# Emformer attention and a pyramid-residual MoE on one core: the first round of dense tiles in two parts

## The chip, the cores and the metric

The kernel runs on one core of one Trainium2 chip. A core has five engines with queues of their own: TensorE (PE, matrix products, with a weight load before each), VectorE (DVE), ScalarE (ACT), GpSimd (POOL) and SyncE (SP). DMA queues are fed by SP, ACT and POOL and share 16 DMA engines. Products are written to PSUM, of which the kernel uses eight banks; everything else on the chip lies in SBUF. The metric is the device time in microseconds of one execution; the kernel before takes 242.95 us, the median of three runs (242.71 to 243.45).

## The reference

```python
def reference(**kwargs):
    attn_out = _attn_ref(q, k, v, mem_k, mem_v)      # (4, 8, 768, 64)
    x = attn_out.transpose(0, 2, 1, 3).reshape(3072, 512)
    return _moe_ref(x, ...)

# attention: 24 chunks of 32 queries; each sees 8 memory keys, 16 keys to the left,
# its own 32 and 8 to the right
scores = scale * np.matmul(q_c, k_full.transpose(0, 1, 3, 2))
a = np.exp(scores - scores.max(-1)); a = a / (a.sum(-1) + 1e-09)
out[:, :, c_start:c_end] = np.matmul(a, v_full)

# MoE: 3072 tokens, width 512, 8 experts of hidden width 512, one expert per token
y_dense = np.maximum(x @ w1_dense, 0.0) @ w2_dense
expert_idx = np.argmax(x @ w_gate, axis=1)
y_moe[mask] = gate_w[mask, None] * (np.maximum(x[mask] @ w1[e], 0.0) @ w2[e])
return y_dense + y_moe
```

`gate_w` is the softmax probability of the chosen expert. All inputs are float32; the kernel loads q, k and the MoE weights as bfloat16.

## The kernel before

**Attention.** The work goes by pairs of heads: 16 pairs `i`, four to a batch `b`. For a pair PE transposes q and k (`transpose_qk`, done two pairs ahead), computes scores of the next pair, transposes the probabilities back (`probs_back`), and multiplies them with the values (`values`, in two halves). DVE takes the maximum and the difference, ACT the exponential; `scaled` (L446) divides by the row sums and so gives x. `gate_part` transposes x (in two PSUM banks), `gate_sum` multiplies it with the gate's weights, `gate_add` sums over the pairs of a batch, and `record` (ACT) writes x as bfloat16 into the batch's records. Values lie in a window layout that needs two copies per pair (`copy_v`, one for each head), on POOL and on DVE or ACT.

**Routing.** When a batch's four pairs are summed, `logits`, `choose`, `ranks` and `rank` find each token's expert and its row in that expert's region of a DRAM tensor `x_reg` (3200 rows for each of 8 experts); `rows_out` (L585, POOL, indirect DMA) writes six times 128 rows there. This runs one or two pairs behind the attention of the next batch. `fill_out` writes 128 pad rows at the start of each region.

**First round.** After three batches at least 11 tiles of 128 rows are whole within their expert. `list_a` (L626, some dozen small DVE steps over 8 counts or 11 x 8 fields) finds where they start and writes it to `src_i`; `bases` (L178) has SP read the list into registers, and `fetch` (L188) has SP load a tile of rows. `transposed` (L199) transposes it on PE into a PSUM bank and copies it on DVE to `xT_of`; `dense_first` (L213, L227) and `dense_second` (L230) are the dense layers, with ACT emptying their banks. In the kernel before, the list stands in pair 15, ahead of that pair's values; the first tile's transposes come after batch 3's logits.

**Second round and experts.** After batch 3's rows `list_b` makes 16 more tiles (20 at most) from the remainders; they go the same way (tiles 11 to 26). Then every tile gets its expert's first layer (`expert_first`, weights copied by DVE to `w_st`, L942) and second layer (`expert_second`, L950), and `out` rows are written by indirect DMA (L964). Seven first layers go ahead of the first second layer, which needs all of `w2_all`.

**Orders.** The order on each engine is written out by hand (`manual_schedule`): instructions of an engine run in the order in which the code issues them, and waits are put in from the data. PSUM tiles named "tp" (`bank`, L101) are two banks used in turn by q and k transposes, `gate_part`, `logits`, `ranks`, `ends` and `transposed`: whoever takes one waits for the reader of the one two before. SP's queue is in order: a fetch that waits holds the fetches behind it. POOL's queue holds weight loads, row writes and copies in order; weights for the second layers are loaded two at a time, the next when the one before the last has landed (L973 to L979), in space that attention's tiles free.

## Time and profile before

| | |
|---|---|
| median of 3 runs | 242.95 us (242.71 to 243.45) |
| the profiled execution's own time | 238.85 us |
| its span | 237.0 us |
| PE busy | 195.5 us, 82% |
| PE weight loads | 146.3 us, 62% |
| DVE busy | 157.2 us, 66% |
| ACT busy | 135.0 us, 57% |
| POOL busy | 145.1 us, 61% |
| DMA | 59879 packets, 38.57 MB |

The profile is of one execution. Its page gives busy times, the span in 40 slices (each digit the busy share in tenths), the chain that ended last and the costliest groups of instructions. A timeline row has start and length in microseconds from the span's start, the engine, the line in the kernel's code, the operation, the tiles written and read, the count, and in brackets the idle time before it and what ended it. "issue" means that nothing the profile shows was waited for. PEld is the weight load, which runs beside products; a queue of an engine has a q behind its name. The first half of the slices is attention, with DMA and DVE near full; from about 129 us on PE is.

### The profile page before, as it was taken

The page shows a single profiled execution, that of the slowest core. Times are in us where ns is not written, and L with a number is a line of the kernel's source. Part 1 is how long each engine was busy: PE and PEld are TensorE (multiplying, and loading weights), DVE is VectorE, ACT ScalarE, POOL GpSimd, SP SyncE. Part 2 cuts the span into 40 slices and gives each one's busy share as a digit, 9 for nine tenths or more (in the row PEclk, how much of TensorE's full clock was granted, in tenths as well). Part 3 has the DMA queues.
Part 4 walks back from the last instruction along what each step waited for, and adds up shares of the span by engine and source line. Part 5 has one row for each costly group of instructions (what it writes and reads, how often), then busy time and mean ns, then how long its engine had stood idle before and what let it go on. Part 6 is the DMA issues. An engine that isn't in the chain of part 4 may idle for free.

```text
span 237.0 us, 7850 instructions
## 1 busy us (share of the span) xinstructions
PE 195.5 (82%) x3147; PEld 146.3 (62%) x3147; DVE 157.2 (66%) x372; ACT 135.0 (57%) x205; POOL 145.1 (61%) x215
## 2 busy tenths in 40 slices
PE   0578787988887888696568999999999899999960
PEld 0467665756666667564336777777778766666630
DVE  4587999879877999877735652222244478888750
ACT  7256676996879678987313555555556433322220
POOL 7939996418996599958312841121232079888880
PEclk9999999999999999999959999999999999999995
DMA  5999999999999999999888569999999324433331
GB/s 87 184 204 129 158 156 188 168 141 166 136 210 206 164 171 198 188 165 278 156 202 140 148 100 250 232 183 187 170 163 148 52 93 175 177 136 127 150 146 76
DMA packets 59879, 38.57 MB, mean 163 GB/s; under 512 B 35646, under 2 KB 57534, under 8 KB 59840
## 3 DMA queue, kind: packets, MB, share of 16 engines
q0 software_dynamic: 21584, 25.20, 58.1%
q1 hardware_dynamic: 37216, 11.77, 28.5%
q10 hardware_dynamic: 1040, 1.06, 1.5%
q8 instruction: 27, 0.44, 0.8%
q14 instruction: 12, 0.10, 0.2%
HBM read 43.22 MB, written 11.30 MB: 230 GB/s over the span
## 4 chain that ended last, share of the span: by engine, by line
POOL 23%; DMA 20%; issue 9%; PE 5%; DVE 5%; ACT 4%; POOLq 1%; ACTq 0%; DVEq 0%
DMA w_all<-in_moe_w_dram 16%; POOL out_dram L964 12%; POOL x_reg L589 5%; POOL idle L583 4%; DMA x_reg<-rec,row_i 2%; DMA xg<-x_reg 2%; PE sc L218 1%; ACT kbd L379 1%; DVE dif L417 1%; DVE mx L411 1%; DVE x L450 1%; DVE kbd L378 1%; ACT qT L374 1%; PE tp L470 1%; PE av L438 1%
## 5 line engine op out<-in xcount | busy, mean ns | idle before, releaser
L589 POOL DMA_INDIRECT x_reg<-rec,row_i x24 | 26.7, 1111 | 20.7 <-ACT rec L480 12.5
L964 POOL DMA_INDIRECT out_dram<-y,dst_i x27 | 29.0, 1074 | 14.3 <-DVE y L960 10.6
L438 PE MATMUL av<-vw,at 128*32 128x130 f32 x768 | 29.1, 284 | 8.5 <-issue 3.9
L438 PEld LDWEIGHTS av<-vw,at 128*32 128x32 f32 x768 | 20.7, 112 | 15.6 <-issue 6.5
L218 PEld LDWEIGHTS <-w_st 128*128 128x128 bf16 x432 | 25.5, 98 | 5.8 <-DVE w_st L942 3.2
L224 ACT ACTIVATE h<-sc 128x512 bf16<-128x512 f32 x27 | 16.1, 597 | 22.8 <-PE sc L218 22.8
L353 POOL COPY vw<-vw 24x1536 f32<-24x1536 f32 x15 | 22.5, 1499 | 9.7 <-DMA vw<-in_v_dram 9.1
L218 PEld LDWEIGHTS <-w1d 128*128 128x128 bf16 x432 | 26.2, 100 | 2.2 <-issue 1.8
L942 DVE COPY w_st<-w_all 128x2048 bf16 x27 | 19.9, 740 | 5.6 <-PE sc L218 4.1
L224 ACT ACTIVATE xT_B<-sc 128x512 bf16<-128x512 f32 x16 | 9.6, 597 | 23.5 <-PE sc L218 23.5
L422 ACT ACTIVATE a<-dif 128x768 f32<-128x768 f32 x16 | 13.5, 845 | 16.0 <-DVE dif L417 13.8
L207 DVE COPY xT_B<-tp 128x512 bf16<-128x512 bf16 x16 | 6.8, 425 | 23.4 <-PE tp L204 23.2
L378 DVE COPY kbd<-tp 64x768 bf16<-64x768 bf16 x16 | 15.2, 948 | 8.0 <-PE tp L365 7.9
L977 POOL CAST scratch<-w_all 1x1 f32<-1x1 bf16 x10 | 1.7, 174 | 28.8 <-DMA w_all<-in_moe_w_dram 28.8
L234 PE MATMUL av<-w2d,h 128*128 128x512 bf16 x72 | 18.5, 379 | 0.0
L430 ACT COPY at<-at_ps 128x768 f32<-128x768 f32 x16 | 12.8, 799 | 7.8 <-PE at_ps L428 7.6
L218 PE MATMUL sc<-xT_B,w_st 128*128 128x128 bf16 x256 | 16.9, 219 | 0.2 <-DVE w_st L942 0.2
L218 PE MATMUL sc<-xT_B,w1d 128*128 128x128 bf16 x256 | 16.9, 219 | 0.0
L411 DVE TENSOR_REDUCE mx<-sc 128x12 f32<-128x768 f32 x16 | 15.3, 956 | 1.7 <-PE sc L401 1.4
L417 DVE TENSOR_TENSOR dif<-sc,mx 128x768 f32<-128x768 f32 x16 | 15.3, 958 | 1.6
L473 ACT COPY xT<-tp 128x384 f32<-128x384 f32 x32 | 13.9, 490 | 3.7 <-PE tp L470 3.7
L450 DVE TENSOR_TENSOR x<-av,rs 128x768 f32<-128x768 f32 x16 | 15.3, 958 | 0.6
(160 smaller groups left out, 449.0 us busy)
## 6 DMA issues: line engine op xcount, KB each, us to landing
w_all<-in_moe_w_dram POOLq DMA_DIRECT2D x14, 512.0 KB, 7.7
vw<-in_v_dram SPq DMA_DIRECT2D x30, 200.0 KB
xg<-x_reg SPq DMA_DIRECT2D x27, 129.0 KB
q_bf<-in_q_dram POOLq DMA_DIRECT2D x16, 192.0 KB, 7.8
k_bf<-in_k_dram POOLq DMA_DIRECT2D x16, 192.0 KB
vw<-in_mem_v_dram SPq DMA_DIRECT2D x32, 48.0 KB
x_reg<-fill ACTq DMA_DIRECT2D x1, 1032.0 KB
w_all<-in_moe_w_dram POOLq DMA_DIRECT2D x4, 256.0 KB, 6.8
```

The lines of the kernel that those rows point to most:

```text
L218: written(place, nc.tensor.matmul(ph[:, f, :], w[:, d, f * 128:(f + 1) * 128], xT[:, d, :], start=(d == 0), stop=(d == DT - 1),))
L224: was_read(place, nc.scalar.activation(h_sb, ph, AF.Relu))
L234: written(place, nc.tensor.matmul(pd, h_d[:, f, :], w2d_sb[:, f, :], start=(f == 0), stop=(f == FT - 1)))
L353: copy(vt[p0 + CHUNK:p0 + CTX, :NCH, hh, :D], vt[p0:p0 + n, 1:, hh, :D])
L378: lo = nc.vector.tensor_copy(dst[:D, 0], srcv[:D])
L411: nc.vector.reduce_max(mx, scv, axis=AX.X)
L417: nc.vector.tensor_tensor(dif.rearrange("p (b t) (h k) -> p b (t h) k", b=2, h=2), scv, mx.to_broadcast([128, 2, T, KEYS]), ALU.subtract,)
L438: nc.tensor.matmul(av[cc * CHUNK:(cc + 1) * CHUNK, t // TB, (t % TB) * W2:(t % TB + 1) * W2], at[:, t, cc * CHUNK:(cc + 1) * CHUNK], vt[:, ...
L450: nc.vector.tensor_tensor(x_p.rearrange("p (b t) (h d) -> p b (t h) d", b=2, h=2), avv[:, :, :, :D], rs.to_broadcast([128, 2, TB * 2, D]), ...
L589: inst = nc.gpsimd.indirect_dma_start(x_reg, bass.IndirectOffsetOnAxis(ap=row_i[:, t:t + 1], axis=0), rec[:, t, :], None,)
L942: nc.vector.tensor_copy(w_st[:, None], w1_all[:, bass.ds(e_dve.pop(s), 1), :, :])
L964: inst = nc.gpsimd.indirect_dma_start(out, bass.IndirectOffsetOnAxis(ap=dst_i[:, s:s + 1], axis=0), y, None, bounds_check=N_tokens - 1, oo ...
```

## The change

- The first round comes in two parts. `list_a` becomes `whole_tiles`, called twice. The first call uses the counts after two batches and gives N1 = 5 tiles; its steps stand in pairs 10, 11 and 12, and the rest of them at the start of pair 15. SP fetches these five in pair 13, before batch 2's row writes in the code, with no order between those rows and these loads. The second call, after pair 15's products, gives tiles 5 to 10.
- `fill_out`'s rows and the fetches of whole tiles have no order between them any more.
- Tiles 0 and 1 are transposed in pair 15 between `probs_back` and `gate_part`; first layers of tiles 0 to 4 stand between the last products of attention and gate, tile 5's transposes and tile 0's second layer ahead of batch 3's ranks. Second layers run three tiles behind the first ones in the first round, and the round's last three end before tile 11.
- `choose` no longer stands behind tile 0's copy on DVE but behind tile 4's; the list is behind `scaled` of the last pair instead of ahead of it.
- The first copy of values for pair 15 moves from ACT in pair 14 to POOL in pair 13, between batch 2's row writes.
- Weights are loaded with four neighbouring rows to a partition, one piece of 8 KB of float32, instead of four rows 128 apart; to match, transposes and first layers read every fourth column. Two weight loads of expert first layers move from the chain at the end to places ahead of and between batch 3's row writes.
- Eight buffers instead of six for fetched tiles, six instead of three for h.

```diff
-    NA, NB, NFIX = 11, 20, 16
+    N1, NA, NB, NFIX = 5, 11, 20, 16
-    m_load = ctx.enter_context(tc.tile_pool(name="m_load", bufs=6))
+    m_load = ctx.enter_context(tc.tile_pool(name="m_load", bufs=8))
...
+    def load_rows(src_ap, dst):
+        nc.gpsimd.dma_start(dst, src_ap.rearrange("(p t) m -> p t m", p=128))
...
-        if s < NA:
-            load_insts.append(inst.ins)
-            for r in row_insts:
+        for b in ((2, 3) if s < N1 else (3,) if s < NA else ()):
+            load_insts[b].append(inst.ins)
+            for r in row_insts[b]:
                 tc.declare_no_dep(
...
+        xk = xgb[:, :D_moe].rearrange("p (m k) -> p k m", k=DT)
         for d in range(DT):
-            nc.tensor.transpose(
-                xtp[:, d, :], xgb[:, d * 128:(d + 1) * 128], identity
-            )
+            nc.tensor.transpose(xtp[:, d, :], xk[:, d, :], identity)
...
+        wk = w.rearrange("p d (m k) -> p d k m", k=FT)
...
-                    ph[:, f, :], w[:, d, f * 128:(f + 1) * 128], xT[:, d, :],
+                    ph[:, f, :], wk[:, d, f, :], xT[:, d, :],
...
-            h_sb = m_work.tile([128, FT, 128], BF16, tag="h", name="h")
+            h_sb = m_work.tile([128, FT, 128], BF16, tag="h", name="h", bufs=6)
...
-    def list_a():
+    def whole_tiles(before, n, cum, first, at):
         cnt = ends()
         ni = r_work.tile([128, E], I32, tag="ni", name="ni")
         nc.vector.tensor_copy(ni, cnt)
+        yield
...
+        yield
...
-        nc.vector.tensor_tensor(src_i[:, :NA], bs, base_a, ALU.add)
+        nc.vector.tensor_tensor(src_i[:, at:at + n], bs, first, ALU.add)
         yield
...
+        if at == 0:
+            nc.vector.tensor_tensor(whole1, reg25, d1[:, :E], ALU.add)
+            nc.vector.tensor_scalar(lim1, whole1, 128.0, None, ALU.mult)
+            step = r_work.tile([128, E], F32, tag="step", name="step")
+            nc.vector.tensor_tensor(step, d1[:, 1:], d1[:, :E], ALU.subtract)
+            nc.vector.tensor_scalar(jump1, step, 128.0, float(ROWS), ALU.mult, ALU.add)
+            nc.vector.scalar_tensor_tensor(
+                base1, d1[:, :1].to_broadcast([128, NA]), 128.0, base_a,
+                op0=ALU.mult, op1=ALU.add,
+            )
...
+            if i == NPAIR - 1:
+                for _ in parts:
+                    pass
...
             probs_back(i)
+            if i == NPAIR - 1:
+                transposed(0)
+                transposed(1)
             gate_part(i - 1)
...
-        if i == NPAIR - 1:
-            parts = list_a()
+        values(i, range(TB))
+        if i in (11, 12):
             next(parts)
-            bases(0, 6)
-            for s in range(6):
-                fetch(s)
-            bases(6, NA)
-        values(i, range(TB))
...
+        if i == NPAIR - 1:
+            dense_first(0)
         if i:
             record(i - 1)
-            if i == NPAIR - 2:
-                copy_v(i + 1, 0, nc.scalar)
...
+        if i == 10:
+            parts = whole_tiles(reg25, N1, cum1, base_a[:, :N1], 0)
+            next(parts)
...
         if i == NPAIR - 3:
-            while rows_todo:
+            bases(0, N1)
+            for s in range(N1):
+                fetch(s)
+            for t in range(T):
                 row_out()
-                if rows_todo:
+                if t == T // 2 - 1:
+                    copy_v(NPAIR - 1, 0, nc.gpsimd)
+                elif t < T - 1:
                     pause()
-            load_w(*w_todo.pop(0))
+            next_w()
...
     last_p = NPAIR - 1
+    next_w()
+    dense_first(1)
     scaled(last_p)
     gate_add(last_p - 1)
+    parts = whole_tiles(whole1, NA - N1, cumA, base1[:, :NA - N1], N1)
+    next(parts)
+    transposed(2)
+    next(parts)
+    next(parts)
+    bases(N1, NA)
+    for s in range(N1, N1 + 3):
+        fetch(s)
     gate_part(last_p)
-    nc.gpsimd.tensor_copy(scratch, xg_of[1][0:1, 0:1])
-    load_w(*w_todo.pop(0))
+    dense_first(2)
+    transposed(3)
+    record(last_p)
     gate_sum(last_p)
-    record(last_p)
     gate_add(last_p)
+    dense_first(3)
+    for s in range(N1 + 3, NA):
+        fetch(s)
+    transposed(4)
     logits(B - 1)
-    transposed(0)
-    dense_first(0)
     choose(B - 1)
-    transposed(1)
-    fetch(6)
-    dense_first(1)
+    dense_first(4)
+    nc.gpsimd.tensor_copy(scratch, xg_of[N1 + 1][0:1, 0:1])
+    next_w()
+    transposed(N1)
+    dense_second(0)
     ranks(B - 1)
     rank(B - 1)
     for t in range(T):
         rows_out(B - 1, (t,))
-        if t < T - 1:
+        if t == T // 2 - 1:
+            next_w()
+        elif t < T - 1:
             pause()
-    dense_second(0)
...
-    for s in range(3, NA):
-        if 4 <= s and s + 5 < NA:
-            fetch(s + 5)
-        if 5 <= s + 1 < NA:
+    for s in range(N1, NA):
+        dense_first(s)
+        if s + 1 < NA:
             transposed(s + 1)
-        dense_first(s)
-        dense_second(s - 1)
-        if s == 5:
+        dense_second(s - 3)
+        if s == N1 + 1:
+            next(parts)
+        if s == N1 + 2:
             for _ in parts:
                 pass
+    for s in range(NA - 3, NA):
+        dense_second(s)
```

`next_w` is `load_rows(*w_todo.pop(0))`. In the second round `dense_second(s - 1)` is left out for the first tile, since the round before has done it.

102 lines of the change are left out of this document (52 added, 50 removed).

## The prediction

> **What bounds the kernel now.** I read the page's head and slices, then busy time by stretch, then the timelines of TensorE (PE), the queues and VectorE (DVE) around the joint of attention and experts.
>
> ```profile
> span 237.0 us, 7850 instructions
> PE   0578787988887888696568999999999899999960
> ```
>
> ```profile
> 118.60:122.00 3.40, 1.72 (x8) 0.48 (x6) 0.42 (x1) 0.75 (x2) 0.00 (x0) 0.50 1.11 229
> 122.00:125.40 3.40, 2.78 (x24) 2.58 (x25) 1.50 (x8) 0.27 (x1) 1.04 (x3) 0.50 0.64 153
> 129.00:146.00 17.00, 17.00 (x208) 12.92 (x207) 8.05 (x45) 9.81 (x17) 9.97 (x20) 1.00 0.70 139
> 150.00:180.00 30.00, 30.00 (x356) 22.31 (x354) 8.47 (x41) 18.14 (x31) 7.34 (x16) 1.00 1.03 177
> ```
>
> The columns are stretch, length, busy PE, weight loads, DVE, ScalarE, GpSimd, granted clock, DMA share and GB/s. From 129 us on PE is full: the end hangs on when it fills and on what is left by then. Before that lies a hole, the slices of 6, 5 and 6, with two stretches at clock 0.50.
>
> ```profile
> 122.10 0.61 PE L204 MATMUL tp<-identity,xg 128*128 128x128 bf16 x4 [1.26 <-DMA xg<-x_reg]
> 123.22 1.86 PE L218 MATMUL sc<-xT_A,w1d 128*128 128x128 bf16 x16 [0.52 <-DVE xT_A L207]
> ...
> 147.00 0.40 PE L204 MATMUL tp<-identity,xg 128*128 128x128 bf16 x4 [0.35 <-DMA xg<-x_reg]
> 147.23 1.06 PE L218 MATMUL sc<-xT_B,w1d 128*128 128x128 bf16 x16
> 148.12 1.03 PE L234 MATMUL at_ps<-w2d,h 128*128 128x512 bf16 x4
> 148.99 0.39 PE L204 MATMUL tp<-identity,xg 128*128 128x128 bf16 x4
> ...
> 188.04 1.02 PE L955 MATMUL av<-w_all,xT_A 128*128 x4 [1.10 <-issue]
> ...
> 228.12 1.02 PE L955 MATMUL at_ps<-w_all,xT_B 128*128 x4
> ```
>
> Start to start, a tile's transposes take 0.23 us, its first dense layer 0.89, its second 0.87. PE waits at 122.10 for tile 0 and at 147.00 for tile 12: both times for rows that went out to x_reg and back. The last product ends at 229.14, the span 7.9 later.
>
> ```profile
> 118.25 0.38 SPq L190 DMA_DIRECT2D xg<-x_reg  x1
> ...
> 139.89 0.33 SPq L190 DMA_DIRECT2D xg<-x_reg  x1
> ```
>
> ```profile
> 128.74 1.04 POOL L589 DMA_INDIRECT x_reg<-rec,row_i  x1 [4.86 <-ACT yd_A L237]
> ...
> 136.26 0.97 POOL L589 DMA_INDIRECT x_reg<-rec,row_i  x1 [0.17 <-issue]
> 137.24 1.62 POOL L115 DMA_DIRECT2D w_all<-in_moe_w_dram  x2
> ...
> 179.73 0.75 POOL L115 DMA_DIRECT2D w_all<-in_moe_w_dram  x1 [0.28 <-issue]
> ```
>
> So a chain is behind PE's second wait: batch 3 routed, six row writes (128.74 to 137.23), fetch of tile 11 at 139.89, tile 12 usable at 147.00. My sum follows this chain, since moving PE work ahead of a wait gains nothing unless the wait ends earlier.
>
> **The change, part by part.**
>
> ```profile
> 89.45 0.95 DVE L378 COPY kbd<-tp 64x768 bf16<-64x768 bf16 x1 [0.21 <-PE tp L365]
> ...
> 95.28 0.95 DVE L378 COPY kbd<-tp 64x768 bf16<-64x768 bf16 x1 [0.20 <-PE tp L365]
> ...
> 102.41 0.95 DVE L378 COPY kbd<-tp 64x768 bf16<-64x768 bf16 x1 [1.30 <-PE tp L365]
> ...
> 109.18 0.96 DVE L450 TENSOR_TENSOR x<-av,rs 128x768 f32<-128x768 f32 x1
> 110.17 1.02 DVE L353 COPY vw<-vw 24x1536 f32<-24x1536 f32 x1
> ...
> 113.17 0.17 DVE L629 CAST ni<-tp 128x8 int32<-128x8 f32 x1 [0.19 <-PE tp L616]
> ...
> 115.70 0.17 DVE L650 TENSOR_TENSOR src_i<-bs,base_a 128x11 int32<-128x11 f32 x1
> ...
> 116.05 0.96 DVE L450 TENSOR_TENSOR x<-av,rs 128x768 f32<-128x768 f32 x1
> ...
> 127.78 0.17 DVE L575 CAST row_i<-rk 128x6 int32<-128x6 f32 x1
> ...
> 128.38 0.42 DVE L207 COPY xT_A<-tp 128x512 bf16<-128x512 bf16 x1 [0.37 <-PE tp L204]
> 128.85 0.42 DVE L207 COPY xT_A<-tp 128x512 bf16<-128x512 bf16 x1
> 129.32 0.24 DVE L653 TENSOR_REDUCE ef<-ind 128x11 f32<-128x88 f32 x1
> ...
> 129.67 0.16 DVE L655 SCALAR_TENSOR_TENSOR lim<-dA,reg 128x8 f32<-128x8 f32 x1
> ```
>
> *Step 1, the early list.* The list of whole tiles is twelve small DVE steps, 113.17 to 115.87, 2.7 us. It now runs twice. The first run stands in pairs 10 to 12, where DVE idles only 0.21 and 0.20 us ahead of the key copies: 2.7 less 0.4 is 2.3 us too much for the gaps. The 1.30 at 102.41 could swallow part of it (low end 2.3 - 1.3 = 1.0), but PE's transposes, for which it waits, hang on ScalarE's copies and so on DVE's own earlier steps. I take 1.7 later from pair 13 on, ends 0.7 (also some covered by narrower arrays) and 2.3.
>
> ```profile
> 110.36 0.82 PE L470 MATMUL tp<-identity_f,x 128*128 128x128 f32 x6
> ...
> 113.18 1.54 PE L438 MATMUL av<-vw,at 128*32 128x130 f32 x48
> ```
>
> *Step 2, the last pair.* x of pair 14 ends at 110.14, now 111.8. Behind it DVE has the copy of v (1.02), the seven left-over steps of the early list (three took 129.32 to 129.83; about 1.1), and the copies of tiles 0 and 1 (0.47 each from 128.38 to 128.85): 114.9. The pair's gate transposes stand behind those tiles' transposes on PE, and both need the same two PSUM banks "tp", which come free with these copies only. So they start near 114.6 instead of 110.36, and values(15) (1.54) ends near 117.0 instead of 114.72. In exchange scaled(15) no longer stands behind the list: x ends at 118.2 against 117.01 now, 1.2 later. That the copy of v leaves ScalarE is worth nothing here, since the banks are later than it.
>
> *Step 3, the late list.* Behind that x come one gate sum, the count, a tile copy and eleven list steps: 0.4 + 0.2 + 0.47 + 2.5, some of it beside x's tail on PE: src_i at about 122.3 (now 115.87).
>
> ```profile
> L353 POOL COPY vw<-vw 24x1536 f32<-24x1536 f32 x15 | 22.5, 1499 | 9.7 <-DMA vw<-in_v_dram 9.1
> ```
>
> ```profile
> L180 SPq TENSOR_LOAD <-src_i x4: 945/1176/2314, 115.9 to 152.4; - x4
> ```
>
> SyncE reads the list into registers (0.95 to 2.31, first time 0.95) and issues the fetch of tile 5 near 123.7; five more fetches are queued behind it. Batch 2's rows don't hold it: they were in by 118.25, plus 1.7, plus the 1.5 us copy of v now between them on GpSimd, is 121.5. By the same 3.85 us as from 118.25 to 122.10, tile 5 is there at 127.5.
>
> *Step 4, routing of batch 3.* Its rank products stand behind tile 5's transposes and the second layer of tile 0: 127.5 + 0.23 + 0.87, and then as before 0.86 from 126.92 (the first rank product) to row_i at 127.78. That is row_i near 129.5, **1.7 later**, although five first layers and a second one are already done. Today the same place waits for tile 0; what is late next is tile 5.
>
> *Step 5, rows and fetch.* From row_i to the last row write's end took 127.78 to 137.23, 9.45. A 0.75 us weight issue replaces one pause of about 0.3: 139.4 against 137.23. The fetch of tile 11 goes 2.66 after it (139.89): 142.1. From fetch to a first layer it took 4.97 at tile 0 (118.25 to 123.22) and 7.34 at tile 11 (139.89 to 147.23), where two weight loads stood ahead. They still do, so the second is nearer in place, but the loads are shorter: I take 5.9. First layer of tile 11 at **148.0**, against 147.23: 0.8 later. PE has by then run out: from 127.5 on six transposes, six first and eleven second layers, 1.4 + 5.3 + 9.6, so at 144 with no stall.
>
> *Step 6, what is left.* From 147.23 to 229.14 stood 81.9 us. Gone from it are the second layer of tile 10 (0.87, now done before) and the 1.10 at 188.04, below: 79.9. PE ends at 227.9, the span 7.9 later at 235.8, **1.2 less**.
>
> *Weights by rows.* Four rows per partition in one piece, eighteen loads.
>
> ```profile
> w_all<-in_moe_w_dram POOLq DMA_DIRECT2D x14, 512.0 KB, 7.7
> ```
>
> From 137.24 to 179.73 twelve loads were issued, two together and then one for each landed: 3.9 us apiece. The last lands 7.7 later, past 187; that is the wait of 1.10. Now ten are left at 139.4. Even at 3.9 the last goes at 174 and lands at 182, before PE asks at about 187. So the faster load itself is put at nothing on the path; the two loads sent earlier take the wait away. Four fewer load instructions in pairs 12 and 13 only bring batch 2's row writes nearer, and by step 3 these don't hold tile 5.
>
> *Fill and fetches of tiles 0 to 4.* They move to pair 13, on a SyncE with no loads left. Nothing waits for them until the last pair; cost nothing, unless they come later than 112. Eight fetch buffers and six h buffers cost space only.
>
> *Strided weight loads.* All first layers (864) and the 108 tile transposes now load weights whose columns lie 8 bytes apart, which no row of before has.
>
> ```profile
> L218 PEld LDWEIGHTS <-w1d 128*128 128x128 bf16 x432 | 26.2, 100 | 2.2 <-issue 1.8
> L428 PEld LDWEIGHTS at_ps<-identity_f,a 128*128 128x128 f32 x96 | 10.8, 146 | 2.9 <-POOL vw L353 1.5 <-ACT a L422 0.4
> ```
>
> Columns 2 bytes apart take 100 ns, 4 bytes apart 146 ns. Products follow each other every 0.89/16 = 56 ns, so a load is hidden up to some length. Bounds: 0, and 972 x 46 ns = 45 us if all of the f32 row's excess showed. I take 0: most of a load lies beside the product before it. A gain is excluded, they are hidden now. [...]
>
> **The sum.** -0.87 - 1.10 + 0.8 = -1.2 us on a span of 237.04 (time of that execution 238.85). The median of the runs, 242.95, is 4.1 above that execution; I carry the difference over: **241.7**. Its own range: fetch to first layer 4.97 to 7.34 and register load up to 2.31 (-0.9 to +2.8), step 1's ends (-1.0 to +0.6): 239.8 to 245.1.
>
> **Rivals.** *The routing is not held.* If the early list fits into gaps, and the late one is done and tile 5 there when PE asks, ranks follow the logits: row_i near 126, fetch of tile 11 near 138.7, first layer at 144.6, 2.6 earlier: 237.04 - 4.6, so 238.4. For it: the removed list ahead of x at 116.05. Against: steps 1 and 2.
>
> *The clock falls (other side).* Between the first round's end (144 to 146) and tile 11 PE may idle 4 us or more. At 118.60 to 125.40, after such a hole, it ran 6.8 us at 0.50, a loss of 3.4. With tile 11 at its late end (2.31 and 7.34: 150.8) the span is 150.8 + 79.9 + 3.4 + 7.9 = 242.0, time 247.9. It is slower from a first layer at about 149.2 on without the clock, from 145.8 with it. Against: stalls on tile copies stretch the first round, so the hole is shorter. [...]
>
> *Strided loads show.* Anything from 244 up to 242.95 + 45 = 288, seen at once in the spacing of first layers; from 1.6 ns each (1.2 us over the 16 first layers, 27 expert first layers and 16 sets of transposes after 147, some 750 loads) it eats the gain.
>
> **How the numbers follow.** The sum's case 0.43, routing not held 0.18, clock 0.18, strided loads 0.13, others 0.08. A measurement can tell 0.3%, 0.7 us, from none. Of the first case 0.27 lies below 242.2, 0.09 within, 0.07 above. Faster 0.27 + 0.18 + 0.03, same 0.09 + 0.03, slower 0.07 + 0.18 + 0.13 + 0.02. The range runs from the second case's 238.4 less a little to just under the third's 247.9; it leaves out most of the strided case.
>
> **What would show it.** Step 1: the key copy at 102.41 about 1.7 later. Step 2: the last pair's gate transposes waiting for tile copies. Step 3 and 4: PE waiting for tile 5 past 125, row_i of batch 3 at 129 to 130. Step 5: a wait for tile 11 or 12 near 146 to 148. Step 6: no wait at the first expert second layer. Weight loads at 98 ns and first layers at 0.89 would clear the strides. It is wrong if row_i of batch 3 comes before 127, if clock 0.50 stands near 147, or if a first layer takes over 0.9.

## The result, and the profile after

The changed kernel takes 250.66 us, the median of five runs, against 242.71 us for the kernel before on the same chip. It is slower by 8.0 us by these medians, where 1.2 us less were forecast, and it lies outside the range. Medians are over all runs, but the ratios of this document leave out disturbed executions, here one of 259.14 us. The ratio is 1.0418, with a 95% interval of 1.0353 to 1.0484.

The profiled execution took 253.21 us with a span of 251.4. It lies 2.5 above its median, while the profiled execution of before lies 3.9 below its own. Part of that gap arose early: when batch 1's row numbers are written (row_i, at 81.44), before any part of the change acts, the changed kernel is already 2.8 us behind the first profile of before (78.68). A second profile of before, experiment 9 below, stands at 81.17 there. So stages are compared, and not times from the start.

The page of the changed kernel, its head, two rows of slices, and from the groups the transposes of tiles (busy time and mean, then the idle time before them and what ended it):

```profile
span 251.4 us, 7852 instructions
PE   0678498877987787692598987599999999999950
PEclk9999979999999999999579999799999999999995
L208 PE MATMUL tp<-identity,xg 128*128 128x128 bf16 x108 | 11.3, 234 | 11.5 <-DMA xg<-x_reg 11.5
```

The hole before the experts has become two, the slices 6, 9, 2, 5 and later 7, 5. PE waited 11.5 us for fetched tiles. Its timeline says where (three dots stand for rows left out):

```profile
114.72 0.87 PE L431 MATMUL at_ps<-identity_f,a 128*128 128x128 f32 x6
121.33 0.62 PE L208 MATMUL tp<-identity,xg 128*128 128x128 bf16 x4 [5.75 <-DMA xg<-x_reg]
122.73 0.62 PE L208 MATMUL tp<-identity,xg 128*128 128x128 bf16 x4 [0.78 <-DMA xg<-x_reg]
123.14 1.63 PE L473 MATMUL tp<-identity_f,x 128*128 128x128 f32 x6
124.70 2.83 PE L441 MATMUL av<-vw,at 128*32 128x130 f32 x48
...
137.40 0.41 PE L208 MATMUL tp<-identity,xg 128*128 128x128 bf16 x4 [0.38 <-DMA xg<-x_reg]
...
154.28 1.03 PE L237 MATMUL at_ps<-w2d,h 128*128 128x512 bf16 x4
159.87 1.04 PE L208 MATMUL tp<-identity,xg 128*128 128x128 bf16 x8 [4.57 <-DMA xg<-x_reg]
161.07 1.86 PE L221 MATMUL sc<-xT_B,w1d 128*128 128x128 bf16 x16 [0.16 <-DVE xT_B L209]
```

Tile 0, which was moved ahead so that it would be there early, is usable at 121.33. Behind its transposes in PE's queue stand the last pair's x transposes (123.14) and last products (124.70), both of them attention's and on the way to batch 3's routing. The second wait, 4.57 us, is for tile 11 at 159.87. The granted clock fell to 0.50 in both waits, from 118.51 to 128.75 and from 159.47 to 162.88, and so is below 1 in the mean of these stretches (it is the third number from the end, behind the busy times of the five engines):

```profile
122.00:129.00 7.00, 6.26 (x74) 5.06 (x74) 2.61 (x9) 0.96 (x2) 0.02 (x1) 0.52 0.98 219
155.00:163.00 8.00, 3.28 (x30) 2.82 (x29) 1.01 (x6) 0.65 (x2) 1.41 (x4) 0.79 1.07 259
```

Why tile 0 was late stands in the timelines of ScalarE's and SyncE's queues, and in the waits of SyncE's queue (what it waited for: total, times, longest):

```profile
107.61 0.42 ACTq L606 DMA_DIRECT2D x_reg<-fill  x1
118.88 2.48 SPq L193 DMA_DIRECT2D xg<-x_reg  x5
```

```profile
SPq L193 <- DMA x_reg<-fill: 16.4, 1, 16.4
SPq L193 <- DMA x_reg<-rec,row_i: 3.2, 2, 2.9
```

The list was in registers at 102.3, and then the fetch of tile 0 waited 16.4 us for the fill of pad rows, from which the change was to free it. The first 5.3 us of that wait passed before the fill was even issued, at 107.61. The last packet of the fill ends at 118.22; the fetch goes at 118.88. The trace's records name the semaphores that these instructions wait on and raise:

```
107.61 ACT  DMA x_reg<-fill    raises 117 when landed
118.77 SP   waits on 117
118.88 SP   DMA xg<-x_reg      raises 117 when landed
119.45 SP   DMA xg<-x_reg      raises 118 when landed
```

By the records of this run the 97 DMAs that SyncE and ScalarE issue raise eight semaphores in turn (108, 110, 111, 113, 114, 116, 117 and 118), and each of them, but for the first one on each semaphore, waits on the one that it is to raise: the fetch until 118.77, 0.55 us after the fill's last packet. The turns are given in another order than the issues in time: between the fill and the first fetch seven loads of values take theirs, so the fetch is the eighth and gets the fill's own. The declared freedom of order took the wait for the data away and left this one. In the kernel before, the two share number 117 too. In its first profile the fill had landed by 117.1 (its last packet ends at 115.11), before the fetch at 118.25; in its second one (9) the fetch waited 1.1 us for the fill.

The second loss is at the row writes of batch 3. GpSimd's timeline, and the fetch of tile 11 in SyncE's:

```profile
140.33 1.04 POOL L592 DMA_INDIRECT x_reg<-rec,row_i  x1 [1.25 <-issue]
...
144.36 0.59 POOL L114 DMA_DIRECT2D w_all<-in_moe_w_dram  x1
...
148.22 0.97 POOL L592 DMA_INDIRECT x_reg<-rec,row_i  x1
```

```profile
153.14 2.96 SPq L193 DMA_DIRECT2D xg<-x_reg  x5
```

From the last row write's issue to the fetch of tile 11 it takes 4.92 us; before it took 3.63 (136.26 to 139.89). The packets of the load issued at 144.36 run from 145.69 to 150.35, in the queue that also carries rows 3 to 5, and no packet of a row starts there between 145.5 and 149.3.

### The profile page after: what moved, and what is told of

Same layout as the page of the kernel before. It is cut to its first block, busy times and chain, and to the rows that moved or that the text cites. A ratio compares the mean times of both kernels' runs of the same rounds, so it can differ in the third digit from the quotient of the medians.

```text
span 251.4 us, 7852 instructions
## 1 busy us (share of the span) xinstructions
PE 199.9 (80%) x3148; PEld 148.9 (59%) x3148; DVE 162.9 (65%) x393; ACT 134.0 (53%) x204; POOL 139.2 (55%) x208
## 4 chain that ended last, share of the span: by engine, by line
POOL 21%; DMA 15%; issue 13%; DVE 8%; PE 8%; ACT 1%; POOLq 0%; SPq 0%; ACTq 0%; DVEq 0%
DMA w_all<-in_moe_w_dram 12%; POOL out_dram L1007 11%; POOL idle L586 4%; POOL x_reg L592 4%; PE av L441 2%; DMA xg<-x_reg 2%; DVE dif L420 1%; DVE mx L414 1%; DVE kbd L381 1%; DMA x_reg<-rec,row_i 1%; PE sc L221 1%; PE tp L473 1%; DVE x L453 1%; PE tp L368 1%; POOL w_all L114 1%
## 5 line engine op out<-in xcount | busy, mean ns | idle before, releaser
L441 PE MATMUL av<-vw,at 128*32 128x130 f32 x768 | 30.6, 297 | 7.0 <-issue 5.0
L356 POOL COPY vw<-vw 24x1536 f32<-24x1536 f32 x16 | 24.2, 1510 | 11.4 <-DMA vw<-in_v_dram 6.9
L221 PEld LDWEIGHTS <-w1d 128*128 128x128 bf16 x432 | 27.2, 115 | 5.4 <-DVE xT_A L209 2.4
L441 PEld LDWEIGHTS av<-vw,at 128*32 128x32 f32 x768 | 21.7, 117 | 12.4 <-issue 9.4
L208 PE MATMUL tp<-identity,xg 128*128 128x128 bf16 x108 | 11.3, 234 | 11.5 <-DMA xg<-x_reg 11.5
L476 ACT COPY xT<-tp 128x384 f32<-128x384 f32 x32 | 14.1, 489 | 10.5 <-PE tp L473 10.5
L208 PEld LDWEIGHTS <-xg 128*128 128x128 bf16 x108 | 8.8, 118 | 15.5 <-DMA xg<-x_reg 12.6
L221 PE MATMUL sc<-xT_B,w1d 128*128 128x128 bf16 x256 | 17.7, 225 | 0.2 <-DVE xT_B L209 0.2
L473 PE MATMUL tp<-identity_f,x 128*128 128x128 f32 x96 | 14.5, 286 | 3.3 <-issue 2.7
```

The costliest lines, as they stand in the source:

```text
L208: nc.tensor.transpose(xtp[:, d, :], xk[:, d, :], identity)
L221: written(place, nc.tensor.matmul(ph[:, f, :], wk[:, d, f, :], xT[:, d, :], start=(d == 0), stop=(d == DT - 1),))
L356: copy(vt[p0 + CHUNK:p0 + CTX, :NCH, hh, :D], vt[p0:p0 + n, 1:, hh, :D])
L441: nc.tensor.matmul(av[cc * CHUNK:(cc + 1) * CHUNK, t // TB, (t % TB) * W2:(t % TB + 1) * W2], at[:, t, cc * CHUNK:(cc + 1) * CHUNK], vt[:, ...
L473: nc.tensor.transpose(xtt[:, t * 128:(t + 1) * 128], xb[:, t0 + t, :], identity_f32)
```

## The experiments

The time of the kernel before depends on the chip, so each kernel is measured beside it on the same one. Chips are lettered; that of the result above has no letter. The numbers are those of the experiments. "The same" is the kernel of the row above it, run again. Where a ratio is missing, the runs were too scattered for one.

| kernel | chip | median, us | before there | ratio, 95% interval |
|---|---|---|---|---|
| 5, changed kernel | A | 252.0 | 247.4 | 1.0187, 1.0070 to 1.0303 |
| 12, changed kernel | C | 251.34 | 240.31 | 1.0484, 1.0421 to 1.0548 |
| 1, fill at the end of pair 15 | A | 248.92 | 247.82 | 1.0201, 1.0048 to 1.0353 |
| 2, fill at the end of pair 14 | A | 248.51 | 247.82 | |
| 13, the same | C | 246.67 | 240.31 | 1.0315, 1.0253 to 1.0377 |
| 3, tiles 0 and 1 behind gate | A | 250.43 | 247.82 | 1.0227, 1.0113 to 1.0341 |
| 17, no load among the rows | D | 251.4 | 252.25 | 0.9936, 0.9854 to 1.0018 |
| 6, as 2, no load among the rows | A | 244.67 | 247.4 | 0.9950, 0.9894 to 1.0007 |
| 15, the same | D | 246.86 | 252.25 | 0.9824, 0.9760 to 0.9889 |
| 10, as 6, old weight layout | B | 242.02 | 240.8 | 1.0069, 1.0022 to 1.0116 |
| 4, before, weights by rows | A | 247.58 | 247.82 | |
| 16, the same | D | 250.0 | 252.25 | 0.9862, 0.9790 to 0.9934 |
| 7, as 2, x transposes first | A | 247.78 | 247.4 | 1.0065, 1.0011 to 1.0118 |
| 8, as 6, x transposes first | A | 245.34 | 247.4 | 0.9962, 0.9913 to 1.0011 |
| 11, as 8, ranks first | B | 240.74 | 240.8 | 0.9963, 0.9919 to 1.0007 |
| 18, the same | D | 244.92 | 252.25 | 0.9728, 0.9671 to 0.9786 |
| 14, as 11, list's rest on GpSimd | C | 240.69 | 240.31 | 1.0018, 0.9986 to 1.0049 |
| 9, kernel before | B | 242.49 | 240.8 | 0.9997, 0.9955 to 1.0039 |

Times alone are blurred by the chip, so stages are read too, between rows that every kernel has: row_i of batches 1, 2 and 3 (b1, b2, b3) on DVE, the first layer of tile 11 (f11), and PE's last product. These are differences of starts in one profile each, and the last column runs to the end of the last product.

| profile | chip | b1 to b2 | b2 to b3 | b3 to f11 | f11 to PE's end |
|---|---|---|---|---|---|
| before, first | | 25.52 | 23.58 | 19.45 | 81.91 |
| before (9) | B | 25.52 | 24.50 | 20.03 | 81.13 |
| changed, first | | 27.83 | 30.10 | 21.70 | 81.44 |
| changed (12) | C | 27.61 | 28.56 | 21.44 | 82.73 |
| changed (5) | A | 30.76 | 24.95 | 22.20 | 85.36 |
| fill in pair 15 (1) | A | 27.49 | 27.58 | 21.48 | 82.66 |
| fill in pair 14 (2) | A | 27.48 | 24.68 | 20.99 | 83.51 |
| the same (13) | C | 27.47 | 24.60 | 21.54 | 81.44 |
| and no load among rows (6) | A | 27.48 | 24.84 | 20.24 | 83.32 |
| the same, old weights (10) | B | 27.69 | 24.53 | 19.09 | 81.88 |
| ranks first (11) | B | 28.24 | 19.79 | 20.39 | 80.57 |
| weights by rows alone (4) | A | 27.60 | 22.80 | 22.62 | 83.78 |

Beside the second profile of before, the changed kernel's first one is 2.3 us longer from b1 to b2, 5.6 from b2 to b3, 1.7 from b3 to f11 and 0.3 from there to PE's end. Behind PE's last product, which the table leaves out, the span goes on for 8.9 us instead of 7.9.

### The shared semaphore

```diff
-        if i == NPAIR - 3:
+        if i == NPAIR - 1:
             fill_out()
```

This is experiment 1; in 2 and 13 it is `NPAIR - 2`.

> The changed kernel with the fill of pad rows issued by ScalarE at the end of pair 15 instead of pair 13. Theory (the fetch of tile 0 waits for the fill, because both raise the same one of eight semaphores in turn, and PE's queue stands behind it): the fetch of tile 0 is issued near 104 instead of 118.88, the PE wait of 5.75 us at 121.33 goes, row_i of batch 3 comes near 129 to 131 instead of 139.37, and the time falls from 250.7 to 240 to 243. Rival (the weights by rows, or the early list on VectorE, make the kernel slower): the fetch may come early, but the time stays above 247. Second rival (the fetch waits for row writes of batch 1 or 2): the fetch stays near 118.

> The changed kernel with the fill at the end of pair 14. In the turn of the eight semaphores it now shares with the fetch of tile 3 instead of tile 0. Theory: fetches of tiles 0, 1 and 2 near 104 to 106, the fetch of tile 3 only when the fill has landed, about 8 to 12 us after its issue, so near 122 to 126; the time lies between 241 and 247. Rival (any other cause of the late fetch: the data of row writes, traffic of the fill on the DMA engines): no jump between the fetches of tiles 2 and 3.

With the fill in pair 15 the five fetches went from 101.43 to 103.98, and the PE wait for tile 0 was gone. But b2 to b3 stayed at 27.58, since PE now waited for tile 5:

```profile
132.44 0.42 PE L208 MATMUL tp<-identity,xg 128*128 128x128 bf16 x4 [3.13 <-DMA xg<-x_reg]
```

From the fetch's issue (128.61) to these transposes it took 3.83 us, against 2.06 in 13, and the fill's packets were running meanwhile (125.81 to 131.61). Whether they made the tile late wasn't tried by itself: in 8, where the fill had landed, the same step took 4.11.

With the fill in pair 14 its turn of the semaphores fell on the fetch of tile 3. SyncE's queue in experiment 2:

```profile
103.27 1.77 SPq L193 DMA_DIRECT2D xg<-x_reg  x3
...
120.31 0.85 SPq L193 DMA_DIRECT2D xg<-x_reg  x2
```

Three fetches at 103 to 104.5, and a jump of 15.8 us to the fourth, a little earlier than the expected 122 to 126: the place of the wait moved with the turn of the semaphore, not with the data or the traffic, which are the same for all five. In experiment 13 its waits name the fill again, and on PE the next wait in line appears:

```profile
SPq L193 <- DMA x_reg<-fill: 16.5, 1, 16.5
```

```profile
116.27 1.01 PE L473 MATMUL tp<-identity_f,x 128*128 128x128 f32 x6 [2.53 <-DVE xT_A L209]
...
151.91 1.04 PE L208 MATMUL tp<-identity,xg 128*128 128x128 bf16 x8 [4.39 <-DMA xg<-x_reg]
```

The fetch that shares goes 0.6 to 0.8 us after the fill's last packet in each of these: 117.25 and 117.87 (12), 117.76 and 118.59 (13), 118.04 and 118.64 (17).

The times on chip A don't show a gain. Experiment 1 was to take 240 to 243 us and took 248.92, on a chip where before took 247.8; by its number the rival, above 247, came true. Its ratio, 1.0201, is no better than the changed kernel's 1.0187 there (5), and the medians, 252.0 and 248.92, were not taken side by side. Experiment 2 missed its 241 to 247 too. The price was measured side by side on two other chips:

> The changed kernel beside the next two on one chip, in more rounds. Theory: 1.02 to 1.04 times before, the fetch of tile 0 within 1 us of the fill's last packet.

> The kernel of the second experiment in more rounds. Theory: the shared semaphore costs 3 to 5 us, so 1.005 to 1.015 times before, and between 0.980 and 0.988 times the changed kernel; what is left over before is the weight load among batch 3's rows (some 1 per cent by the sixth experiment). Rival: the semaphore costs little in the time, and this kernel stays within 1 per cent of the changed one.

On chip C 251.34 against 246.67: 4.7 us by the medians, 4.1 by the ratios (1.0484 - 1.0315, of 240.3). On chip D, without the load among the rows, 251.4 against 246.86 (17 and 15): 4.5 by the medians, 2.8 by the ratios. On these two chips the rival "little in the time" falls. But both ratios came out above what was expected: 13 is still 1.0315 times before, so more than half of the loss on that chip is elsewhere.

Experiment 3 left the late fetch and moved PE's work instead.

```diff
-            if i == NPAIR - 1:
-                transposed(0)
-                transposed(1)
             gate_part(i - 1)
...
     gate_part(last_p)
+    transposed(0)
+    transposed(1)
+    dense_first(0)
+    dense_first(1)
```

> The changed kernel with the transposes of tiles 0 and 1 and the first layers of tiles 0 and 1 moved behind the last pair's products and its x transposes; the fill stays in pair 13. Theory: the fetch of tile 0 still goes near 118, but PE's queue no longer holds attention's last products behind it: gate transposes of pair 14 before 117, row_i of batch 3 near 129 to 132, time 242 to 246. Rival (weights by rows or the early list): time stays above 248.

Half right. The x transposes of pair 14 came at 116.06, and b2 to b3 is 27.02, against 28.56 and 30.10 in two profiles of the changed kernel. In the third, 5 on the same chip, it is 24.95, but there the 3 us stand in the stage ahead (30.76). Row_i of batch 3 came at 135.92 instead of 129 to 132. The time stayed at 250.43, so by its number the rival, above 248, came true. PE's wait at tile 11 was 3.52 us, and the clock ran 6.8 us at half behind it. To take the wait away from PE's queue is not enough.

### The load among batch 3's rows

```diff
         rows_out(B - 1, (t,))
-        if t == T // 2 - 1:
-            next_w()
-        elif t < T - 1:
+        if t < T - 1:
             pause()
```

> The fill at the end of pair 14, as in the second experiment, and the weight load in the middle of batch 3's row writes given back to the chain behind them. Theory (that load's packets lie ahead of rows 3 to 5 in one queue, which costs some 1.3 us of the wait from the last row to the fetch of tile 11, and its issue 0.4 us): from the last row write's issue to the fetch of tile 11 about 3.7 us instead of 5.06, row_i to the first layer of tile 11 near 19.3 instead of 20.99, and the time 1.0 to 2.0 us below the second experiment's kernel. Rival (the larger weight packets of the earlier loads or of the two loads behind the rows make the wait longer): the 5.06 stays, the time with it.

> The kernel of the sixth experiment in more rounds: fill at the end of pair 14, no weight load among batch 3's rows. Theory (the mid load is the second cause; in the thirteenth experiment tile 11 was waited for 4.39 us, and the clock fell behind it): 1.002 to 1.012 times before, against 1.0315 with the load. Rival (what is left is the price of weights by rows, and the old layout alone brought the tenth experiment to 1.0069): 1.02 to 1.03.

> The changed kernel without the weight load among batch 3's rows; the fill stays where it shares its semaphore with the fetch of tile 0. Theory (two causes that add: 1.6 per cent for the semaphore, 2 to 2.5 for the load): 1.02 to 1.03 times before. Rival (they overlap, PE waits at tile 11 either way): 1.035 to 1.045.

In 6 and 15 this edit comes on top of the fill in pair 14, in 17 it is made alone in the changed kernel. The four ratios on chip D, here, for the weights and for the ranks below, all came out under what was expected; the kernel before takes 252.25 us there.

The time fell: 247.78 to 245.34 between kernels 7 and 8 on chip A, which differ in this load alone. That is 2.4 us by the medians, 2.5 by the ratios, and 1.3 by the medians of the runs that enter the ratios. Between 2 (four runs) and 6 it was 248.51 to 244.67. Tile 11 was no longer waited for in 6, 15 and 17.

The detail of the expectation was wrong on chips A and D. The fetch came 5.7 to 5.9 us after the last row instead of 3.7, because there the second list on DVE was late (below): in 15 it was written at 144.22, the fetch 2.6 later. On chip B, where the list was early, it took 2.95 us in 10 (139.52 to 142.47) and 3.20 in 11, against 4.86 in 13 on chip C. 10 differs from 13 in the weight layout and the chip too, 11 in the order of the ranks and the chip. The changed kernel itself wasn't run on chip D, so whether the two causes add can't be told from 17; PE's wait for tile 0 is in it as in the changed kernel:

```profile
PE tp L208 <- DMA xg<-x_reg: 6.2, 2, 5.8
```

### The weights

> The kernel before with nothing but the weights by rows: one 8 KB piece per partition, and transposes and first layers that read every fourth column. Theory: first layers still 0.89 us apart, weight loads 114 to 118 ns instead of 98 to 101, the 1.10 us wait at the first expert second layer gone; time within 2 us of before, so 240.5 to 244. Rival (the strided reads or the larger weight packets cost the time): 246 to 251.

> The kernel of the fourth experiment in more rounds: the kernel before with weights by rows alone. Theory (its loads slow pairs 12 and 13 by up to 2 us, and its wait of 1.10 us less gives some back): 0.998 to 1.008 times before. Rival (the strided reads or the loads are a main cause): 1.015 to 1.03.

```diff
-                src_ap[t * 128:(t + n) * 128].rearrange("(t p) m -> p t m", p=128),
+        nc.gpsimd.dma_start(dst, src_ap.rearrange("(p t) m -> p t m", p=128))
...
-                xtp[:, d, :], xgb[:, d * 128:(d + 1) * 128], identity
+            nc.tensor.transpose(xtp[:, d, :], xk[:, d, :], identity)
...
-                    ph[:, f, :], w[:, d, f * 128:(f + 1) * 128], xT[:, d, :],
+                    ph[:, f, :], wk[:, d, f, :], xT[:, d, :],
```

This is made in the kernel before, with whole loads in place of its halves; experiment 10 makes the same step backwards in kernel 6, and there the loads stay whole. By itself it isn't slower: no difference can be seen on chip A, and it is 1.4% faster on D. The 247.58 us of 4 lie in its rival's range, but before took 247.82 there. The wait at the first expert second layer was 0.31 in 4; but it was 0.36 in the second profile of before too, and 0.33 in 10 with the old layout, so the 1.10 of the first profile is not what the layout takes away. First layers are 0.89 us long from start to start also in the changed kernel (139.56 to 140.45). Rows of its page:

```profile
L221 PEld LDWEIGHTS <-w1d 128*128 128x128 bf16 x432 | 27.2, 115 | 5.4 <-DVE xT_A L209 2.4
L221 PE MATMUL sc<-xT_B,w_st 128*128 128x128 bf16 x256 | 17.0, 220 | 0.3 <-DVE w_st L985 0.3
w_all<-in_moe_w_dram POOLq DMA_DIRECT2D x16, 512.0 KB, 6.7
```

A strided load takes 115 ns instead of 100 and stays hidden; products last 220 instead of 219; weights land 6.7 us after issue instead of 7.7. The 8 KB of the expectations is the length of a piece in float32; in the records a weight packet holds 4096 bytes (1024 in the kernel before).

> The kernel before once more, to see its stages in a second profile. From row_i of batch 1 to row_i of batch 2 its first profile took 25.52 us; all kernels with the weights by rows took 27.5 to 27.8 there. Theory (the 8 KB weight packets of pairs 12 and 13 hold attention's loads up for 2 us): 25.5 again. Rival (chip and execution): 27 or more here too.

> The kernel of the sixth experiment (fill at the end of pair 14, no weight load among batch 3's rows) with weights, tile transposes and first layers as in the kernel before: rows 128 apart, contiguous columns. Theory (weights by rows cost 2 us in pairs 12 and 13 and give little back): row_i to row_i of batches 1 and 2 near 25.5, time 1 to 2 us below the sixth experiment's 0.995 times before. Rival (they cost nothing there, and give the 1.10 us wait at the first expert second layer): 27.5 again, and the time equal or up to 2 us above it, 0.995 to 1.005 times before.

Attention between b1 and b2 takes 25.52 us in both profiles of before and 27.5 to 27.8 in nearly all others (28.24 in 11, 30.8 in 5 and 7). The loads by rows alone do that (27.60), and so does the early list with the old layout in whole loads (27.69); together they don't add (27.48). The rival of experiment 9, chip and execution, falls; the theory of experiment 10 falls as well, since the old layout doesn't give 25.5 back; its ratio, 1.0069, is even a little above its rival's 0.995 to 1.005. What the two have in common is that loads are whole instead of in halves; whether that is the cause wasn't tried.

### What is late next

```diff
             probs_back(i)
-            if i == NPAIR - 1:
-                transposed(0)
-                transposed(1)
             gate_part(i - 1)
+            if i == NPAIR - 1:
+                transposed(0)
+                transposed(1)
```

> The fill at the end of pair 14, and pair 14's x transposes ahead of the transposes of tiles 0 and 1 on PE. Theory (the x transposes wait for the two PSUM banks that the tiles' copies on VectorE free late, 2.79 us at 118.71): the wait of 2.79 goes; row_i of batch 3 comes 1.5 to 2.5 us earlier than the 133.83 of the second experiment, counted from row_i of batch 2 (24.68 there), and the time falls by 1 to 2.5 us. Rival (VectorE's own queue sets x of pair 15 and so the list): the wait moves to the tiles' transposes, row_i stays within 0.5 us, and so does the time.

> The fill at the end of pair 14 with both edits of the two kernels before it. If both theories hold their gains add: 2.0 to 4.5 us below the second experiment's kernel, 0.98 to 0.995 times before. If VectorE sets the order, only the load's 1 to 2 us are won: 0.99 to 1.0 times before.

The wait for the tiles' copies was there, and to remove it gave nothing. In experiment 8 the x transposes no longer wait for copies, and PE waits for tile 5 instead:

```profile
114.69 0.85 PE L473 MATMUL tp<-identity_f,x 128*128 128x128 f32 x6 [0.86 <-DVE x L453]
115.84 0.77 PE L208 MATMUL tp<-identity,xg 128*128 128x128 bf16 x8 [0.29 <-ACT xT L476]
...
130.23 0.41 PE L208 MATMUL tp<-identity,xg 128*128 128x128 bf16 x4 [2.40 <-DMA xg<-x_reg]
```

b2 to b3 is 25.51 there against 24.84 in 6, the time 245.34 against 244.67. So the rival of experiment 7 holds, and of 8's two gains only that of the load came.

```diff
     dense_first(4)
-    nc.gpsimd.tensor_copy(scratch, xg_of[N1 + 1][0:1, 0:1])
-    next_w()
-    transposed(N1)
-    dense_second(0)
     ranks(B - 1)
     rank(B - 1)
+    dense_second(0)
+    transposed(N1)
...
-        if s == N1 + 1:
+        if s == N1:
             next(parts)
-        if s == N1 + 2:
+        if s == N1 + 1:
             for _ in parts:
```

> The kernel of the eighth experiment (fill at the end of pair 14, x transposes first, no load among the rows) with batch 3's rank products and row numbers ahead of tile 5's transposes and tile 0's second layer, no weight load ahead of the rows, and the second list one tile earlier. Theory (PE's queue holds routing behind tile 5, which arrives late: 2.40 us of wait and 1.1 us of products): row_i of batch 3 comes 3 us earlier (22.5 after that of batch 2 instead of 25.51), tile 11's first layer 2 to 4 us earlier, and the time falls to 0.975 to 0.99 times before. Rival (PE is full by then, so earlier rows only bring tiles that wait): row_i earlier, time within 1 us of the eighth experiment's, 0.992 to 1.0 times before.

> The kernel of the eleventh experiment in more rounds. Theory: 0.992 to 0.998 times before. Rival: no difference that can be measured, 0.998 to 1.004.

With the ranks ahead of tile 5, b2 to b3 falls from 25.51 (8, chip A) or 24.53 (10, chip B) to 19.79 (11, chip B), and on chip D from 24.51 (15) to 21.65 (18). Row_i of batches 2 and 3 in experiment 11:

```profile
108.99 0.17 DVE L578 CAST row_i<-rk 128x6 int32<-128x6 f32 x1
128.78 0.17 DVE L578 CAST row_i<-rk 128x6 int32<-128x6 f32 x1
```

This is the best version. Its routing came even earlier than the theory has it, its time on chip B as the rival has it: it can't be told from the kernel before (0.9963, interval up to 1.0007). Beside the profile of 9 on the same chip, routing (b2 to b3) gains 4.7 us; 2.7 are lost again in b1 to b2, and 1.5 behind PE's last product, where the span goes on for 9.4 us instead of 7.9. Why it does is open. On chip D it is 2.7% faster than before and 0.8% below kernel 15, whose interval it overlaps a little.

> The kernel of the eleventh experiment with the last seven steps of the early list off VectorE's path: six small ones on GpSimd behind batch 2's rows, the two for the experts' numbers behind batch 3's. Theory (VectorE is full until x of the last pair, so each step there costs its length): x of pair 15 and the late list 0.8 to 1.3 us earlier, counted from row_i of batch 2, and 0.988 to 0.994 times before. Rival (the late list isn't what PE waits for): no change against the eleventh experiment's 0.9963.

```diff
-            nc.vector.tensor_tensor(whole1, reg25, d1[:, :E], ALU.add)
-            nc.vector.tensor_scalar(lim1, whole1, 128.0, None, ALU.mult)
+            nc.gpsimd.tensor_tensor(whole1, reg25, d1[:, :E], ALU.add)
+            nc.gpsimd.tensor_scalar(lim1, whole1, 128.0, None, ALU.mult)
...
```

This puts the list's leftover steps on GpSimd. It brought nothing, as the rival has it: 1.0018 on chip C, no better than 11's 0.9963 on B.

> The changed kernel once more, on the same chip as the next three. Both theories: 1.03 to 1.045 times before; the fetch of tile 0 between 117 and 120, at the landing of the fill.

The repeat of the changed kernel on chip A, 1.0187, was below the expected range; the kernel before takes 247.4 us there. Its fetch of tile 0 went at 116.42, a little early too.

## Why the prediction was wrong

**The step that failed** is "Fill and fetches of tiles 0 to 4 ... move to pair 13 ... Nothing waits for them until the last pair; cost nothing, unless they come later than 112". They came at 118.88. I took the declared freedom as the end of the wait and looked for data and queues only; the semaphore that the fill and the fetch of tile 0 share was not priced, though it is the same in the kernel before. The step names its own condition, and the condition failed. It cost 4.1 to 4.7 us on chip C, 2.8 to 4.5 on D, and can't be told on A. All later times of the prediction shift with it: tile 5 was to be there at 127.5 and was transposed at 137.40; row_i of batch 3 was to come at 129.5 and came at 139.37. Of these 9.9 us each, 2.8 were there at row_i of batch 1 already, ahead of the change.

**Step 5 was mis-sized.** From row_i to f11 I had 18.5 us. It took 21.70, and 21.54 with the fill out of the way (13). The rows took 9.8 us, as forecast, and so the load's issue is small. Its packets in the rows' queue weren't counted: from the last row's end to the fetch it took 3.95 where I had 2.7. The fetch to first layer took 7.93 where I had 5.9, longer than the upper bound of 7.34. The load costs 1.3 to 2.5 us (7 to 8). Half of my rival "the clock falls" came true with it: PE ran out at 155.3, waited 4.57 us, and the mean clock between 155 and 163 was 0.79. In the changed kernel's profile the clock fell at 118.51 and 159.47, within PE's gaps of 5.75 and 4.57 us. It fell behind shorter gaps as well: at 33.18 in the same profile behind one of 2.71, in 13 at 117.43 behind one of 2.53, and in the first profile of before at 118.62 with none above 2.02 us just ahead (PE was busy for 1.17 of the 3.42 us before it). So the 0.50 that the rival was taken from didn't follow "such a hole" of 4 us; that a hole of this length brings a fall was my estimate, and no run here shows from which length on the clock falls.

**Step 1 was right in size.** From the fourth last key copy to the last it took 18.87 before and 20.42 after (87.00 to 107.43), 1.6 later, where 1.7 was taken. The reason given, the list's steps, isn't shown: weights by rows alone give 20.16 (4).

**Step 2 was right and hidden.** In the changed kernel the late tile covers the wait for the banks. Without it the x transposes wait 2.53 us for the copies (13), 11.1 us after the last key copy, where 10.5 was forecast. But to remove it was worth nothing in the time (8 against 6).

**Steps 3 and 4 were one us short,** apart from the semaphore. With the fill in pair 14 b2 to b3 is 24.6 to 24.7. The prediction has 105.9 to 129.5, 23.6. Two profiles of before differ by as much there (23.58 and 24.50). That tile 5 is late next was right: 2.40 in 8, and the ranks ahead of it gain 2.9 (15 to 18, D) to 4.7 (10 to 11, B) in that stage.

**Step 6 came near its number, in part by luck.** From f11 to PE's end it took 81.44, of which 1.8 us were still at half clock (161.07 to 162.88), 0.9 lost: 80.5 without, where 79.9 was forecast. PE's first expert second layer waited 0.34 instead of 1.10, but the second profile of before has 0.36 there. So the term of 1.10, the largest one of the sum, was read from one execution, and most of it was no gain of the change. The span behind PE's end, which I carried over as 7.9, was 8.9. **Strided loads** were rightly put at nothing in the time, since first layers are still 0.89 us apart. The load itself takes 15 ns more (115 instead of 100), and these stay hidden.

With the fill moved and the load taken out, the kernel is close to before and not clearly below it on chip B: 1.0069 in 10, with the old weights, and 0.9963 in 11 with the ranks moved as well. On chip D, where before takes 252.25 us, 15 and 18 are below it. So the gain of 1.2 us that the sum promised isn't shown on a chip like that of the first measurement, even without the two faults.

The stages of 10 against 9 on the same chip are 2.2 longer, equal, 0.9 shorter and 0.8 longer; the prediction's steps come to 1.7 longer, equal, 1.0 shorter and 2.0 shorter. Of the missing 2.8 in the last one, 1.1 is the wait, which 9 doesn't have either (0.36 against 0.33 in 10). Another 1.7 is the clock: in 10 it stood at 0.50 for the first 3.4 us from f11 on (150.14 to 153.56), with PE busy throughout. In 11 it did not, and the stage is 0.6 shorter (80.57 against 81.13), where 0.9 for tile 10's second layer is left of the forecast.

## What to carry to other kernels

Before a transfer is counted as free, list everything that its queue waits for ahead of it, the reuse of completion semaphores included: here the fetch, the eighth DMA behind the fill in the turn, waited 16.4 us for these 1032 KB, with no order of data between the two, and PE's wait of 5.75 us for that tile held all that stood behind it in PE's order. Work that is put ahead as a filler holds up what stands behind it when its data are late, as tile 5 did for 3.13 us in 1 and 2.40 in 8. The big load in the middle of the chain of small writes on one queue was paid in the landing of the last write, not in its issue: the rows took the 9.8 us of the forecast, and from their end to the fetch it took 3.95 instead of 2.7. And a wait that stands in one profile may be gone in the next one of the same kernel, as the 1.10 us at the first expert second layer, 0.36 in the second profile: look at a second profile before a term of the sum rests on it.

## What the runs showed of the hardware that was not expected

The same kernel before took 240.3 to 240.8 us on chips B and C, 247.4 to 247.8 on A and 252.25 on D; the changed one took 250.7 to 252.0 on three chips. Part of what differs shows in the profiles: on A and D PE, ScalarE and VectorE stand still together at one place of the first round, in kernels without a weight load among the rows. In experiment 15:

```profile
138.31 1.08 PE L221 MATMUL sc<-xT_A,w1d 128*128 128x128 bf16 x16 [1.50 <-issue]
142.40 0.60 ACT L227 ACTIVATE h<-sc 128x512 bf16<-128x512 f32 x1 [3.22 <-remote]
142.40 0.42 DVE L209 COPY xT_A<-tp 128x512 bf16<-128x512 bf16 x1 [2.13 <-remote]
142.88 1.08 PE L221 MATMUL sc<-xT_A,w1d 128*128 128x128 bf16 x16 [2.40 <-DVE xT_A L209]
```

ACT and DVE start again at the same instant, and the views name no releaser. By the records both wait for semaphore 115, which PE raises. PE's first layer, transposes and second layer of that place are recorded as ended at 139.39, 139.62 and 140.48, but their three raises come together, at 142.31 to 142.43. In experiment 10 on chip B the raises of the same three follow the recorded ends within 0.1 us (138.78, 139.00 and 139.87). In 6, 17 and 18 they come some 2 to 3 us behind the ends as well. So it is PE's products, or the reports of them, that came late there. From row_i of batch 3 to the second list it takes 11.5 to 12.9 us in 4, 6, 8 and 15 to 18, and 8.0 to 9.7 in 9 to 13 on B and C. What holds PE up stays open, and so does whether it is what slows the kernel before on A and D, since no profile of that kernel was taken there.

The turn of eight semaphores cost SyncE's queue 16.4 us of waiting in the changed kernel, 16.2 in 12 and 16.5 in 13; no run here shows what would happen without the wait.
